# A spectral mixing block with one routed token: W's last rows by one gather, the second group's half columns on GpSimd, and seven even buffers against eight of two sizes

## The chip, the cores and the metric

The kernel runs on one core of one Trainium2 chip. Its time is the device time of one execution in microseconds: 198.0 us is the median of three runs (197.77 to 198.25). The profile is one further execution: it took 199.04 us, of which 197.4 us are the span from the first to the last instruction. Engines are called by their short names in the profile: PE (matmul), DVE (vector), ACT (scalar), POOL (GpSimd), SP (the queue that issues most loads).

## The reference

One layer over 2048 tokens of 576 numbers, all in float32:

```python
def _layernorm(x, axis=-1, eps=1e-5): ...
# mixing: Real(DFT over tokens (DFT over columns)), by dense matrices
a = einsum("bsd,ed->bse", x, dft_hid_re)
b = einsum("bsd,ed->bse", x, dft_hid_im)
y = einsum("ts,bse->bte", dft_seq_re, a) - einsum("ts,bse->bte", dft_seq_im, b)
h = x + y                          # with layernorm(x) going in
# routed part: one token, a SwiGLU of width 4608
r = layernorm(h) @ w_r
idx = argsort(-r)[:, :1]
y = (silu(x_sel @ w_gate) * (x_sel @ w_up)) @ w_down * sigmoid(r_sel)
h2 = h + layernorm(h) + (y in the row of the token)
```

The two pairs of DFT matrices are inputs like any other (2 x 16.8 MB over the tokens, 2 x 1.3 MB over the columns), and so are the three matrices of the routed part (10.6 MB each).

## The kernel before, in words

**The symmetries and their check.** The kernel computes the mixing with a part of the matrices, as far as they are mirror images of themselves, and it checks on the chip that they are: it reads the mirrored parts too, subtracts or adds, squares the differences and sums the squares. If the sum is not near zero, a general path (never taken here) computes all from new. So nearly all of the matrices is loaded, and the check is work for DVE and ACT. The token matrix ("ct") comes in blocks of 128 columns by row group j (0 to 8, and 16 - j), by part i (0 real, 1 imaginary), "plain" with nine column tiles (128 partitions x 9 x 128 float32, 576 KB) and "mirrored" with seven (448 KB, gathered in reverse order by GpSimd with an indirect load). The column matrix ("wt", called W) comes in five row blocks of 128; rows 0 to 287 are needed plain and the others mirrored.

**The stages.** X is loaded, folded and normalized (0 to 30 us). Then two groups of row groups, GROUPS = [[1,2,3,4,5],[6,7,0,8]], go through the same steps: `seq` (matmuls with ct, PE), `keep` (PSUM to the tile Z, ACT and DVE), `hid` (matmuls with W, PE), `residual` and `dot_h` (add to X, product with w_r, DVE), `spread_of` (variance, ACT), `scores` (small DVE work for each batch of tokens), `result` (rows of the output, ACT and POOL) and stores by POOL. When the scores of all tokens are known, `top`, `spread`, `token` and `row_of_token` find the token and put its row, normalized, into PSUM and into the tile `xs`. Then come the routed part's products: 9 blocks of w_gate and w_up, each with four rows of 576 a partition, are multiplied with that row on POOL (`products_on_pool`, 14 of them), DVE and ACT (sums), and PE multiplies with w_down (`down`, tile pd). `last_of_row` finishes the token's row and ACT stores it.

**The checks.** `c_check(j, i)` waits for a plain and a mirrored block of row group j and of 16 - j, and forms the differences on DVE in a half of the tile Q: `off_s` (two of 128 x 896) and `off_t` (128 x 1152). `c_half` does the same for the half columns (`off_h`: of a group's plain blocks, the left half of each column tile against the right half), for two row groups at a time. `off_w` does it for W. ACT then squares the half of Q (`square`, line 368) and frees it. Q has two halves, handed out in the order in which the checks stand in the program.

**Places.** Plain blocks that `seq` uses have fixed places in the tile D (D0, D1, D2). All others (the mirrored ones, and the plain ones of 16 - j) take the next free of the "raw" places: seven in the tile R of nine column tiles each, and those units of D that are not in use. A place is free again when DVE has read it. Loads of plain blocks are issued by SP, mirrored ones by POOL, each queue in its own order and at most eight in flight. Later the same memory is cut into 16 buffers for the blocks of the routed part (R's places 0 and 1, 2 and 3, 4 and 5 make one each).

**What sets the order.** Every step is an entry with an engine, an estimated duration and its dependencies; a list scheduler (`Plan.order`) simulates them and the instructions of each engine are written in the order that comes out, the longest remaining way first. Which place a load takes is set earlier, by the order in which `ring` is called. So a changed estimate or place moves instructions on all engines. The routed part's loads are planned over six passes, each to the buffer that is free first.

In the lines: 301 is POOL's gather, 357 SP's load of a plain block, 375, 380 and 387 are `off_s`, `off_t`, `off_h` on DVE, 403 and 405 the load of W, 422 to 427 `off_w`, 619 and 623 `residual` and `dot_h`, 661 `result`, 1200 a load of the routed part, 1228 a product on POOL, 1255 `down`. The changed kernel has the same steps some 10 to 50 lines lower: its gathers are line 311, its loads of ct 372 and of W 420 and 422, its `off_h` is 406, its squares are 383 and its `result` is 692.

## Time and profile before

| what | value |
|---|---|
| median of three runs | 198.0 us |
| the profiled execution, and its span | 199.04 us, 197.4 us |
| busy: PE, DVE, ACT, POOL | 66%, 84%, 71%, 59% of the span |
| moved by DMA | 77.81 MB, 394 GB/s over the span |

The profile gives the busy time of each engine, the chain of work that ended last, groups of equal instructions, and the DMA's rate in 40 slices or in stretches of one's choice. In the timeline a row has the start, the duration (both in us), the engine, the line of the program, and the tiles out<-in with their shapes; what stands in brackets is the idle time before the instruction and who ended it. "DMA share" is the mean busy share of the 16 DMA engines, GB/s what they moved: both are high when large transfers run, a low share means that nothing was queued, and a high share at a low rate means that the engines were busy with something that moves little.

### The profile page before, as it was taken

The numbers are of one execution on the slowest core, as the hardware profiler recorded it, in microseconds if no ns is written. First come the engines' busy times: TensorE is split into PE (matmuls) and PEld (weight loads), VectorE is DVE, ScalarE is ACT, GpSimd is POOL, SyncE is SP. The second block draws the span as 40 slices with busy tenths as digits, with TensorE's granted clock in tenths as the row PEclk, the third lists the DMA queues.
The fourth block names the chain that finished last, engine by engine and source line by source line (L and its number), as shares of the span: only waits on it lengthen the run. The fifth ranks groups of instructions, "written<-read, shape, count | busy, mean of one in ns | idle before, by whom it ended". The sixth has DMA issues, their size and how long they took to land. (4 is left out here: it accounts for less than half of the span.)

```text
span 197.4 us, 2794 instructions
## 1 busy us (share of the span) xinstructions
PE 129.6 (66%) x758; PEld 89.9 (46%) x758; DVE 166.6 (84%) x419; ACT 140.4 (71%) x259; POOL 117.2 (59%) x139
## 2 busy tenths in 40 slices
PE   0007999999999999799999986900232036263940
PEld 0005667754667788477876764700121013031430
DVE  4399996999899968999799999999947999989720
ACT  3198853684699578799389399889555999877630
POOL 6488888284637876359780000003874999999900
PEclk9999999999999999999999999975555555558797
DMA  5999999999899999999999999999999999999992
GB/s 171 408 418 412 413 409 406 411 381 330 281 405 411 411 363 402 400 410 411 416 405 414 418 424 420 426 422 412 424 431 425 420 428 424 422 431 414 412 427 99
DMA packets 14587, 77.81 MB, mean 394 GB/s; under 512 B 1951, under 2 KB 1955, under 8 KB 11239
## 3 DMA queue, kind: packets, MB, share of 16 engines
q1 hardware_dynamic: 10461, 56.56, 71.5%
q0 software_dynamic: 4096, 21.03, 26.5%
q8 instruction: 7, 0.11, 0.2%
q14 instruction: 13, 0.11, 0.1%
q10 hardware_dynamic: 10, 0.00, 0.0%
HBM read 72.86 MB, written 6.49 MB: 402 GB/s over the span
## 5 line engine op out<-in xcount | busy, mean ns | idle before, releaser
L368 ACT ACTIVATE Q<-Q 128x2944 bf16<-128x2944 bf16 (+5 forms) x26 | 55.4, 2132 | 18.5 <-DVE Q L380 8.9
L610 PE MATMUL py<-W,Z 128*128 128x289 f32 x180 | 45.4, 409 | 3.8 <-DVE X L619 3.8
L565 PE MATMUL ps<-D,XF 128*128 128x320 f32 (+3 forms) x216 | 45.0, 408 | 0.5 <-DVE Z L583 0.5
L301 POOL DMA_INDIRECT R<-in_ct_dram,ic x21 | 32.1, 1528 | 17.7 <-DVE Q L375 13.5
L610 PEld LDWEIGHTS py<-W,Z 128*128 128x128 f32 x180 | 33.6, 189 | 15.2 <-issue 4.5
L565 PEld LDWEIGHTS ps<-D,XF 128*128 128x128 f32 (+1 forms) x216 | 32.0, 172 | 13.0 <-issue 1.5
L1228 POOL TENSOR_TENSOR D<-D,Z 128x1152 f32<-128x1152 f32 x8 | 20.9, 2642 | 0.0
L676 POOL DMA_DIRECT2D out_dram<-X x1 | 0.6, 621 | 32.1 <-ACT X L661 32.1
L301 POOL DMA_INDIRECT D<-in_ct_dram,ic x11 | 13.8, 1250 | 7.6 <-DVE Q L380 4.6
L498 ACT ACTIVATE junk<-X,XT 128x576 bf16<-128x576 f32 x16 | 12.3, 771 | 7.8 <-DMA X<-in_x_dram 3.3
L1233 ACT ACTIVATE junk<-D 128x576 bf16<-128x576 f32 x20 | 13.7, 683 | 3.2 <-POOL D L1228 2.6
L1255 PE MATMUL pd<-XF,H 128*1 128x144 f32 x80 | 5.3, 439 | 14.6 <-DVE H L1247 11.3
L537 PE MATMUL fo<-W,diag 128*128 128x288 f32 (+1 forms) x8 | 4.2, 706 | 16.3 <-DVE diag L528 16.3
L375 DVE TENSOR_TENSOR Q<-R,D 128x896 bf16<-128x896 f32 x11 | 11.9, 1084 | 3.2 <-DMA D<-in_ct_dram 1.8
L387 DVE TENSOR_TENSOR Q<-D 128x640 bf16<-128x640 f32 (+3 forms) x20 | 12.8, 691 | 1.7 <-DMA W<-in_wt_dram 1.7
L380 DVE TENSOR_TENSOR Q<-R,D 128x1152 bf16<-128x1152 f32 x10 | 13.4, 1348 | 0.0
L630 ACT ACTIVATE junk<-X,TD 128x576 bf16<-128x576 f32 x16 | 12.3, 766 | 1.4 <-DVE X L619 1.3
L661 ACT ACTIVATE X<-X,BB,UP 128x576 f32<-128x576 f32 x14 | 10.8, 854 | 3.1 <-DVE BB L642 3.1
L623 DVE SCALAR_TENSOR_TENSOR junk<-X,wr 128x576 bf16<-128x576 f32 x16 | 12.1, 755 | 0.3
L375 DVE TENSOR_TENSOR Q<-D 128x896 bf16<-128x896 f32 x11 | 11.8, 1082 | 0.0
L619 DVE SCALAR_TENSOR_TENSOR X<-py,X 128x576 f32<-128x576 f32 x16 | 11.6, 748 | 0.0
L375 DVE TENSOR_TENSOR Q<-R 128x896 bf16<-128x896 f32 x10 | 10.7, 1082 | 0.1
(205 smaller groups left out, 260.8 us busy)
## 6 DMA issues: line engine op xcount, KB each, us to landing
D<-in_ct_dram SPq DMA_DIRECT2D x22, 576.0 KB
R<-in_ct_dram SPq DMA_DIRECT2D x10, 576.0 KB
D<-in_wu_dram SPq DMA_DIRECT2D x5, 1152.0 KB
D<-in_wd_dram SPq DMA_DIRECT2D x4, 1152.0 KB
R<-in_wg_dram SPq DMA_DIRECT2D x3, 1152.0 KB
D<-in_wg_dram SPq DMA_DIRECT2D x3, 1152.0 KB
out_dram<-X SPq DMA_DIRECT2D x2, 1440.0 KB
X<-in_x_dram SPq DMA_DIRECT2D x4, 576.0 KB
```

Source lines behind the costliest of these rows:

```text
L301: pool.indirect_dma_start(tile, None, view, bass.IndirectOffsetOnAxis(ap=rows, axis=0), element_offset=at)
L368: act.activation(t, t, AF.Square, accum_out=DS[0 : t.shape[0], n : n + 1])
L375: dve.tensor_tensor(o, C[j, i, True][:, 0:7, :], C[j, i, False][:, 7:0:-1, :], op=SIGN[i])
L380: dve.tensor_tensor(o, C[NK - j, i, False], C[j, i, False][:, :, ::-1], op=SIGN[i])
L387: dve.tensor_tensor(o[:, :, k::2, :], t[:, :, k::2, 0:HM], t[:, :, k::2, HM:P], op=op)
L498: act.activation(junk[:, 0:D], X[:, k, 0:D], AF.Square, bias=XT[:, n : n + 1], scale=-float(D), accum_out=VX[:, n : n + 1],)
L565: pe.matmul(cm(ZP[g, n][k % 2][p0 : p0 + m], w), XF[:, q, m0 : m0 + m], DT[g, i][:, :, k, 0:HM], start=k in (0, 1), stop=k in (6, 7),)
L610: pe.matmul(YP[GROUPS[g][c]][:, h, 0:w], Z[:, a, c * P : (c + 1) * P], w_block(a)[:, h * HD : h * HD + w], start=(a == 0), stop=(a == 4),)
L623: dve.scalar_tensor_tensor(junk2, X[:, k, 0:D], 1.0, wr, op0=OP.mult, op1=OP.mult, accum_out=TD[:, n, 0:1])
L630: act.activation(junk[:, 0:D], X[:, k, 0:D], AF.Square, bias=TD[:, n, 1:2], scale=-float(D), accum_out=VAR[:, n : n + 1],)
L1228: pool.tensor_tensor(t, t, xs.unsqueeze(1).to_broadcast([P, JW, D]), op=OP.mult)
L1233: act.activation(junk[:, 0:D], WB[w, j][:, r, :], AF.Copy, accum_out=acc[:, j + r : j + r + 1])
```

## The change

Four things, and what follows from them.

1. **W's last block.** W's plain blocks now hold rows 1 to 128 and 129 to 256 instead of 0 to 127 and 128 to 255. The rest (rows 0 and 257 to 288, plain and mirrored) comes as one gather of 128 half rows of 576 numbers, with a table of row numbers in five small POOL instructions, and two half rows by SP. Before, it was a load of 33 rows, one of 32 half rows, and later a gather of 33 mirrored rows. The check of this block is a new function, `off_wc`. A clearing of the block's tile at the start of the program falls away; so does a clearing of one entry of the old table. The layout of the folded X shifts by one column to fit.
2. **The second group's half columns.** `off_h` of the second group runs on GpSimd.
3. **Eight raw places in the same 63 column tiles.** Three have nine column tiles (0 to 2) and five have seven (3 to 7). A plain block takes only a place of nine; a mirrored one takes a place of seven or a unit of D first.
4. **Two places closed early.** From the check of row group 7, part 0, on, places 0 and 1 of R get no more loads of ct.

A gather of nine entries before a store, which turns the order of the DMA engines, becomes one of four.

```diff
-N_RAW = 7
+N_RAW, N_MAIN = 8, 3
...
+LEFT = {(7, 0): (0, 1)}
...
+        pool.memset(iw[:, 2:3], 0)
+        for c in range(2):
+            for p, n, row, step in ((0, 32, D1, 2), (32, 31 + c, D - D1, -2)):
+                pool.iota(iw[64 * c + p : 64 * c + p + n, 2:3], pattern=[[0, 1]], base=2 * row + c, channel_multiplier=step)
...
-        return RAW[:, b]
+        if b < N_MAIN:
+            return RAW[:, b]
+        at = LOW + (b - N_MAIN) * 7 * P
+        return RF[:, at : at + 7 * P].rearrange("p (k m) -> p k m", m=P)
...
+    def half_on_pool(g, c, i):
+        return g == 1
...
-            dve.tensor_tensor(o[:, :, k::2, :], t[:, :, k::2, 0:HM], t[:, :, k::2, HM:P], op=op)
+            eng = pool if half_on_pool(g, c, i) else dve
+            eng.tensor_tensor(o[:, :, k::2, :], t[:, :, k::2, 0:HM], t[:, :, k::2, HM:P], op=op)
...
-            rows = wt[n * P : n * P + (P if n < 2 else 33), :].rearrange("p (c e) -> p c e", c=2)
-            sp.dma_start(t if n < 2 else t[0:33], rows)
-            if n == 2:
-                sp.dma_start(W[name][64:96, 0, 0:D], wt[2 * P : HD, D : 2 * D])
...
+        elif n == 2:
+            sp.dma_start(W["C"][0:2, 1, 0:D], wh[1 : D + 2 : D, :])
...
+        else:
+            gather(W["C"][:, 0, 0:D], wh, iw[:, 2:3])
...
+    def off_wc(u):
+
+        c, o = W["C"][:, 0, :], Q[:, u % 2, 0 : D + 289]
+        dve.memset(o[:, 0:D], 0.0)
+        for p, op in ((0, OP.subtract), (64, OP.add)):
+            dve.tensor_tensor(o[p : p + 31, 0:D], c[p + 32 : p + 63, 0:D], c[p : p + 31, 0:D], op=op)
+        dve.tensor_copy(o[32:34, 0:D], W["C"][0:2, 1, 0:D])
+        off_e(o[:, D:], c[0:64], c[64:P])
...
-    dve.memset(W["C"], 0.0)
...
-        u = free.pop(0)
+        open_ = [b for b in free if b not in shut]
+        whole = [b for b in open_ if type(b) is tuple or b < N_MAIN]
+        u = whole[0]
+        if f == load_c and args[2]:
+            u = [*[b for b in open_ if type(b) is tuple or b >= N_MAIN], *whole][0]
+        free.remove(u)
...
-            add("DVE", 0.16 + 0.62 * m, then(off_h, g, c, m, i, u), [d for _, d in cus[i]], w)
+            add(
+                *(("POOL", 0.3 + 1.31 * m) if half_on_pool(g, c, i) else ("DVE", 0.16 + 0.62 * m)),
+                then(off_h, g, c, m, i, u), [d for _, d in cus[i]], w,
+            )
...
-    for step in "sffsffwsss":
+    for step in "sffsffwcsss":
```

The rows below are the instructions of an engine in program order; "x3" stands for three alike in a row. First SP's loads after those of X, before the change (R and D are the tiles of the places, W the column matrix):

```order
L357 DMA D<-in_ct_dram 128x1152 x10
L357 DMA R<-in_ct_dram 128x1152 x2
L357 DMA D<-in_ct_dram 128x1152
L403 DMA W<-in_wt_dram 128x2x576 x2
L403 DMA W<-in_wt_dram 33x2x576
L405 DMA W<-in_wt_dram 32x576
L357 DMA D<-in_ct_dram 128x1152
L357 DMA R<-in_ct_dram 128x1152 x2
L357 DMA D<-in_ct_dram 128x1152 x2
```

and after it:

```order
L372 DMA D<-in_ct_dram 128x1152 x10
L372 DMA R<-in_ct_dram 128x1152 x3
L420 DMA W<-in_wt_dram 128x2x576 x2
L422 DMA W<-in_wt_dram 2x576
L372 DMA D<-in_ct_dram 128x1152
L372 DMA R<-in_ct_dram 128x1152 x2
L372 DMA D<-in_ct_dram 128x1152 x2
```

The two small loads of W have become one of two rows. The four plain blocks for which a place is free from the start are the same in number, three of them now in R. The eighth place goes to a mirrored block: POOL has eight gathers into places that are free from the start where it had seven.

Second, DVE at the end of the second group, before the change (py is the sum of `hid`, X the residual stream, wr is w_r; Q<-D are the half columns):

```order
L623 SCALAR_TENSOR_TENSOR junk_126,TD<-X,wr 128x576 x2
L375 TENSOR_TENSOR Q<-D 128x896
L387 TENSOR_TENSOR Q<-D 128x2x5x64
L387 TENSOR_TENSOR Q<-D 128x2x4x64
L619 SCALAR_TENSOR_TENSOR X,TD<-py_1_799,X 128x576 x2
L387 TENSOR_TENSOR Q<-D 128x2x5x64
L387 TENSOR_TENSOR Q<-D 128x2x4x64
L619 SCALAR_TENSOR_TENSOR X,TD<-py_2_818,X 128x576
```

and POOL after it, from its last gather of ct to the first store of results (on DVE the half columns of this group are gone):

```order
L311 DMA spare<-in_x_dram,ix 4x2
L406 TENSOR_TENSOR Q<-D 128x2x5x64
L406 TENSOR_TENSOR Q<-D 128x2x4x64
L406 TENSOR_TENSOR Q<-D 128x2x5x64
L406 TENSOR_TENSOR Q<-D 128x2x4x64
L406 TENSOR_TENSOR Q<-D 128x2x5x64
L406 TENSOR_TENSOR Q<-D 128x2x4x64
L406 TENSOR_TENSOR Q<-D 128x2x5x64
L406 TENSOR_TENSOR Q<-D 128x2x4x64
L707 DMA out_dram<-X 128x1728
```

All eight instructions stand on POOL between its gathers and its stores. 

Third, ACT at the same place, before the change (Q,DS<-Q is a square of a half of Q, the last two those of the half columns):

```order
L368 ACTIVATE Q,DS<-Q 128x2304
L630 ACTIVATE junk,VAR<-X,TD 128x576
L368 ACTIVATE Q,DS<-Q 128x2304
L630 ACTIVATE junk,VAR<-X,TD 128x576
L240 ACTIVATE SD<-VAR,eps 128x6
L661 ACTIVATE X<-X,BB,UP 128x576 x14
L1056 TENSOR_LOAD cit
```

and after it:

```order
L383 ACTIVATE Q,DS<-Q 128x2304
L661 ACTIVATE junk,VAR<-X,TD 128x576
L692 ACTIVATE X<-X,BB,UP 128x576 x4
L661 ACTIVATE junk,VAR<-X,TD 128x576
L250 ACTIVATE SD<-VAR,eps 128x6
L692 ACTIVATE X<-X,BB,UP 128x576 x6
L383 ACTIVATE Q,DS<-Q 128x2304
L692 ACTIVATE X<-X,BB,UP 128x576 x4
L1106 TENSOR_LOAD cit
```

The first square now stands ahead of the first four results and the last root (SD), the second one ahead of the last four results; TENSOR_LOAD is the start of `row_of_token`.

More of the change, by code (lines that the diff above doesn't have):

```diff
@@ L877, in w_first, with wc_first @@
             LAST["SP"], d = load(
-                "SP", then(load_w, None, n), (0.59, 0.59, 0.22)[n], LAST["SP"], users["W" + "ABC"[n]]
+                "SP", then(load_w, None, n), (0.59, 0.59, 0.005)[n], LAST["SP"], users["W" + "ABC"[n]]
             )
             WL.append(d)
+    def wc_first():
+        LAST["POOL"], d = load("POOL", then(load_w, None, 5), 0.295, LAST["POOL"])
+        WC.append(d)
     def w_check():
-        for n in range(3):
-            u, d = ring("POOL", load_w, (0.59, 0.59, 0.16)[n], n + 3)
+        for n in range(2):
+            u, d = ring("POOL", load_w, 0.59, n + 3)
             q, w = qs.take()
@@ L887, in w_check, with wc_check @@
             users[u].append(o)
-            squares(q, 3 * D, o, W_ROWS[n])
+            squares(q, 3 * D, o)
             WS.append(o)
             free.append(u)
+    def wc_check():
+        q, w = qs.take()
+        WS.append(add("DVE", 2.6, then(off_wc, q), WL[2], WC, w))
+        squares(q, D + 289, WS[-1])
     ZU = {(-1, False): users["Z"], (-1, True): users["Z"]}
@@ L1010 @@
         for j in GROUPS[1]:
+            shut.update(LEFT.get((j, i), ()))
             c_check(j, i)
```

88 lines of the change are left out of this document (50 added, 38 removed).

## The prediction

> **What bounds the kernel now.** I read the DMA's rate by stretches first, since the page shows the DMA engines busy in nearly every slice. The columns are the stretch and its length, five engines' busy time with instruction counts, PE's granted clock, the mean busy share of the DMA engines, and GB/s.
>
> ```profile
> 35.00:44.00 9.00, 9.00 (x38) 5.79 (x36) 9.00 (x16) 6.97 (x6) 5.40 (x2) 1.00 1.03 400
> 44.00:48.00 4.00, 4.00 (x31) 1.99 (x29) 3.48 (x5) 2.00 (x5) 0.94 (x1) 1.00 1.04 288
> ...
> 50.50:54.00 3.50, 3.50 (x15) 2.47 (x14) 2.55 (x5) 2.91 (x3) 2.26 (x2) 1.00 0.81 237
> 54.00:72.00 18.00, 18.00 (x74) 13.41 (x73) 16.09 (x19) 15.13 (x18) 11.92 (x9) 1.00 1.02 410
> 72.00:75.00 3.00, 3.00 (x15) 2.65 (x14) 2.40 (x9) 2.04 (x3) 2.26 (x3) 1.00 1.03 316
> ...
> 100.00:150.00 50.00, 29.48 (x132) 20.58 (x131) 45.52 (x125) 37.85 (x61) 13.17 (x24) 0.80 1.01 420
> 150.00:187.50 37.50, 16.61 (x230) 8.19 (x230) 34.68 (x96) 31.61 (x88) 36.30 (x14) 0.58 1.01 422
> 187.50:193.00 5.50, 2.15 (x65) 1.62 (x64) 1.09 (x7) 1.55 (x5) 0.00 (x0) 1.00 1.02 420
> 193.00:195.00 2.00, 0.00 (x0) 0.00 (x0) 0.00 (x0) 0.00 (x0) 0.00 (x0) 1.00 0.38 138
> ```
>
> The loads run at 400 to 422 GB/s without a pause until 193 us, but for three places. In two of them (44 to 48 and 72 to 75 us) the engines are busy and move little. In the third (50.5 to 54) the share falls to 0.81: nothing was queued. So the stream of loads is a bound, and it can be shortened at those three places.
>
> Then the end, from the timeline: POOL's first and last product, PE's last instructions, the token's row and its store.
>
> ```profile
> 151.10 2.62 POOL L1228 TENSOR_TENSOR XF<-XF,Z 128x1152 f32<-128x1152 f32 x1 [2.91 <-ACT Z L1103]
> 184.73 2.67 POOL L1228 TENSOR_TENSOR D<-D,Z 128x1152 f32<-128x1152 f32 x1
> 190.56 1.16 PE L1255 MATMUL pd<-W,H 128*1 128x144 f32 x32
> 191.79 0.37 DVE L1268 SCALAR_TENSOR_TENSOR orow<-pd,sg,orow 97x144 f32<-97x144 f32 x1 [1.91 <-PE pd L1255]
> 192.30 1.12 ACTq L1278 DMA_DIRECT2D out_dram<-orow  x1
> ```
>
> Between the first product and the last POOL is busy 36.30 of 37.50 us (row 150 to 187.5 above): the 14 products stand end to end. They start when the token's row is there (the wait for ACT, Z), and the row's store follows the last of them by 192.30 - 187.40 = 4.9 us. So there is a second bound: the time at which the token is known, call it the token's time (151.1 us), plus 46.3 us. It ends together with the stream of loads. A gain needs both; the smaller of the two gains is what the end shows.
>
> **The stream of loads.** These are the issues of W's loads (SP's row of three includes the one of 33 rows; POOL's is the mirrored gather of 33 rows).
>
> ```profile
> 30.57 2.38 SPq L403 DMA_DIRECT2D W<-in_wt_dram  x3
> 64.21 0.94 POOL L301 DMA_INDIRECT D<-in_wt_dram,iw  x1 [0.30 <-issue]
> 70.64 0.76 DVE L422 TENSOR_TENSOR Q<-R,W 128x576 bf16<-128x576 f32 x1 [1.82 <-DMA R<-in_wt_dram,iw]
> 95.14 1.09 DVE L375 TENSOR_TENSOR Q<-R,D 128x896 bf16<-128x896 f32 x1 [1.77 <-DMA D<-in_ct_dram]
> 41.72 9.63 SPq L357 DMA_DIRECT2D R<-in_ct_dram  x2
> ```
>
> The gather of W's first mirrored block, issued two gathers ahead of that at 64.21, ends DVE's wait at 70.64; the small one, one gather later, falls into 72 to 75. The small plain loads are the last of W behind a queue that was some ten microseconds long, and fall into 44 to 48. I take both slow stretches to be the transfers with 33 rows. The first moved 4.0 x 288 = 1.152 MB, which at 410 GB/s takes 2.81 us: 1.19 us lost. The second moved 0.948 MB, 2.31 us: 0.69 lost. The change replaces them by a gather of 128 even rows, of the kind that ran at 410 between 54 and 72 us, and a load of two. In bytes it removes two times 33 x 1152 and 32 x 576 numbers and adds 130 x 576: 378 kB against 300 kB, 0.19 us. Sum: 1.19 + 0.69 + 0.19 = 2.07 us. The bounds are 0.2, if the slow stretches have another cause, and 2.07, if the two-row load costs nothing visible.
>
> The first 1.19 us are not safe by themselves. SP's row at 41.72 shows two loads that took 9.63 us to issue: the places were full until DVE had read them, and from 50.5 the queue was empty. If W's loads end 1.0 us earlier (1.19 less the part of the new gather, which is now issued here), the queue is empty that much earlier. But the eighth place lets one more mirrored block be fetched ahead: 128 x 896 x 4 bytes = 0.459 MB, 1.12 us at 410. It pays for just that. So the hole at 50.5 (0.83 MB in 3.5 us, 1.48 us lost) should stay as it is, and I count nothing for it; its bounds are 1.48 won and some 1.2 lost. That a plain block finds only three places in R is no restriction at first: each check takes two mirrored and one plain block and gives back the same.
>
> **The token's time.** DVE is busy without a gap from 117 us to the scores; these are its costliest groups there (busy us, mean ns).
>
> ```profile
> L623 DVE SCALAR_TENSOR_TENSOR junk<-X,wr 128x576 bf16<-128x576 f32 x15 | 11.3, 755 | 0.3
> L387 DVE TENSOR_TENSOR Q<-D 128x640 bf16<-128x640 f32 (+1 forms) x8 | 5.6, 753 | 0.0
> L619 DVE SCALAR_TENSOR_TENSOR X<-py,X 128x576 f32<-128x576 f32 x4 | 2.9, 753 | 0.0
> L1228 POOL TENSOR_TENSOR D<-D,Z 128x1152 f32<-128x1152 f32 x8 | 20.9, 2642 | 0.0
> L676 POOL DMA_DIRECT2D out_dram<-X x1 | 0.6, 621 | 32.1 <-ACT X L661 32.1
> ```
>
> The half columns leave DVE: 8 instructions, 5.6 us, some 5.4 us after the overlap of neighbours. The row of L1228 (this and the next are from the page) prices them on POOL: 2642 ns for 1152 elements of two inputs, and a pair of 640 and 512 has as many, so four pairs take 10.6 us. POOL stood idle for 32.1 us between its last gathers and its first store (L676), so there is room for them once the last checks have freed the halves of Q.
>
> How much the two disturb each other no row shows for two large instructions. The nearest are a gather on POOL beside DVE's checks, and one without:
>
> ```profile
> 88.20 4.33 POOL L301 DMA_INDIRECT R<-in_ct_dram,ic  x1 [0.30 <-issue]
> 101.56 0.94 POOL L301 DMA_INDIRECT D<-in_ct_dram,ic  x1 [0.30 <-issue]
> 88.35 1.08 DVE L375 TENSOR_TENSOR Q<-D 128x896 bf16<-128x896 f32 x1
> 89.36 1.34 DVE L380 TENSOR_TENSOR Q<-R,D 128x1152 bf16<-128x1152 f32 x1
> 90.62 1.08 DVE L375 TENSOR_TENSOR Q<-R 128x896 bf16<-128x896 f32 x1
> 91.63 0.74 DVE L583 SCALAR_TENSOR_TENSOR Z<-ps,os 128x256 f32<-128x256 f32 x2
> ```
>
> The gather ended at 92.53, 0.90 after DVE went from instructions with two inputs in SBUF to one that reads PSUM: POOL had stood still for 3.4 us. DVE's own durations do not show a loss there. So POOL can be held off by DVE; whether a large POOL instruction holds off DVE is the open price. Its bounds: nothing, and all of POOL's 10.6 us less the 2.9 us of L619, which reads PSUM: 7.7 us. I take half, 3.9 us, since every entry of L623 ends with a short readout at which POOL can get in and then hold the next. The half columns thus win 5.4 - 3.9 = 1.5 us (from 5.4 won to 2.3 lost).
>
> The Trainium skill (SBUF — State Buffer, section "SBUF: two separate sides") says that VectorE and GpSimd have one pair of ports in common, that an instruction takes it whole, and that a VectorE instruction with two SBUF inputs takes it against a GpSimd one that reads SBUF. By that rule the upper bound of 7.7 us is the price, and the token's time is 2.3 us later from this edit alone; the trace agrees as far as POOL stood still for 3.4 us.
>
> Upstream, DVE waited 1.77 us at 95.14 for a load that the shorter stream brings some 2 us earlier, and has no gap behind it: up to 1.8 us. The token's time should come 1.5 + 1.8 = 3.3 us earlier, more than the 2.07 of the loads. So the loads set the gain.
>
> **What is hidden.** `off_wc` has two instructions of 31 x 576, a clearing and a copy where `off_w` had two of 33 x 576; rows of the old block and of a clearing of 288 numbers:
>
> ```profile
> 76.97 0.74 DVE L422 TENSOR_TENSOR Q<-D,W 33x576 bf16<-33x576 f32 x1
> 79.04 0.14 DVE L427 CAST Q<-W 33x1 bf16<-33x1 f32 x1
> L698 DVE MEMSET XF<- x1: 298/298/298, 1.5 to 1.5; 128x288 f32 x1
> 10.15 0.13 POOL L222 IOTA ti<- 128x1 int32 x1
> 15.06 0.24 POOL L484 TENSOR_TENSOR DX<-X 128x4 f32<-128x4 f32 x1 [0.52 <-DMA X<-in_x_dram,ix]
> ```
>
> The same with 0.30 and a copy of at most 0.74 added: up to 1.0 us on DVE. DVE's wait at 95.14 hides it; without that cover the token is 1.0 later, which 3.3 allows. The five instructions for the new table (0.13 each, 0.65 us, one old one of the kind less) end in POOL's wait of 0.52 us at 15.06; the rest is far ahead of the first place that matters. Placing: loads of the routed part wait for D places that now POOL frees; the stream had no gap from 100 to 193 us (rows above), and a few microseconds are in its queue.
>
> **Sum.** 197.4 - 2.07 = 195.3 us of span. The execution lies 1.64 us above its span, at 199.04, and the median 1.04 below that; against the median it is 198.0 - 2.07 = 195.9, and with 0.1 for the last load, which is now two halves of 576 KB and leaves PE twice as much to do behind it, **196.0 us**.
>
> **The rivals.**
> - *The hole fills too.* The eighth place fetches far enough ahead, and 1.48 us more are won: 198.0 - 3.55 = 194.5. For it: the share of 0.81 is only a lack of places. Against it: DVE, which frees them, is busy throughout, and the token's time must come 3.5 us earlier as well.
> - *What W gives, the hole takes.* The queue is empty earlier, and the extra block is not fetched in time, since SP still waits for places in its order: only 0.69 + 0.19 = 0.88 remain, 197.1. With the lock at three quarters of its bound it comes to about the same.
> - *GpSimd and VectorE shut each other out (slower).* Each half column on POOL stops DVE's products of L623. This costs the token 7.7 - 5.4 = 2.3 us. Beside that, ACT's second square of the half columns now stands ahead of the last four results and of the token's row, and waits for POOL:
>
> ```profile
> 124.38 2.12 ACT L368 ACTIVATE Q<-Q 128x2304 bf16<-128x2304 bf16 x1 [0.19 <-DVE Q L387]
> 141.86 3.14 ACT L661 ACTIVATE X<-X,BB,UP 128x576 f32<-128x576 f32 x4 [2.40 <-DVE BB L642]
> ```
>
>   If POOL ends after 139.7, its 2.12 us delay the results. Together 4.4 us less the 1.8 from upstream, or none of it: 0.5 to 2.8 later, 199.6 in the middle. It decides from the point where POOL's eight instructions cost DVE and ACT more than 5.4 + 1.8 = 7.2 us together. Against it: DVE's instructions that read PSUM, and its waits, let POOL in.
> - *The places do not do what they say:* a plain block waits for one of three places, new holes between 55 and 100 us eat it all: 198.0.
>
> **How the numbers follow.** Forecast 43%, the hole filled 13%, the hole takes 20%, shut out 18%, places 6%. A measurement of this kernel tells 0.2%, 0.4 us, from no change. Faster: 43 + 13 + two thirds of 20, 69%. Same: 7 of the 20 and 5 of the places, 12%. Slower: 19%. The likeliest case's own range is 195.2 to 196.9; with the others 194.3 to 199.2.
>
> **What would show it.** Right: no stretch near 44 and 72 us with a full share and under 380 GB/s; a hole of about 1.5 us near 50; POOL's first product 2 us or more earlier; the stream at full rate to 191. Wrong: eight L406 that take more than 13 us in all with L654 longer than 755 ns; a first product later than 151.1; shares under 0.95 between 55 and 105 us.

## The result: 1.3% slower, and the profile after

| what | before | after |
|---|---|---|
| median, six runs of each | 198.24 us | 201.2 us |
| ratio after to before, 95% interval | | 1.0128 (1.0093 to 1.0163) |
| profiled execution, and its span | 199.04 us, 197.4 us | 200.27 us, 198.5 us |
| POOL's first product | 151.10 us | 152.72 us |
| moved by DMA | 77.81 MB | 77.74 MB |

The forecast was 196.0 us, from 194.3 to 199.2. The profiled execution of the changed kernel was the fastest of its six, so its trace shows 1.1 us of span more, where the medians are 3.0 us apart. Here and below the ratio leaves out executions in a slower state that most versions show now and then (203.39 us here), so it is not the ratio of the two medians.

The DMA's rate by stretches in the changed kernel, with the columns of the prediction:

```profile
35.00:44.00 9.00, 9.00 (x39) 5.90 (x39) 8.48 (x15) 7.39 (x8) 5.46 (x5) 1.00 1.03 406
44.00:48.00 4.00, 4.00 (x29) 2.02 (x26) 4.00 (x6) 1.08 (x4) 0.88 (x1) 1.00 1.01 393
50.50:54.00 3.50, 3.50 (x15) 2.47 (x14) 2.55 (x5) 3.50 (x3) 2.18 (x2) 1.00 1.01 388
54.00:70.00 16.00, 16.00 (x65) 11.85 (x64) 15.93 (x20) 13.75 (x17) 9.74 (x4) 1.00 1.02 409
70.00:82.00 12.00, 11.35 (x50) 9.13 (x49) 9.97 (x21) 6.84 (x14) 8.56 (x8) 1.00 0.98 343
120.00:125.00 5.00, 5.00 (x16) 3.58 (x16) 5.00 (x8) 3.38 (x8) 2.22 (x2) 0.74 0.65 234
150.00:190.00 40.00, 17.32 (x231) 8.22 (x230) 35.80 (x98) 32.48 (x90) 36.27 (x14) 0.58 1.01 421
```

and two of these stretches before the change:

```profile
70.00:82.00 12.00, 12.00 (x54) 10.07 (x54) 10.76 (x23) 9.79 (x16) 6.28 (x6) 1.00 1.02 383
120.00:125.00 5.00, 3.26 (x14) 2.25 (x13) 5.00 (x12) 4.75 (x11) 0.00 (x0) 1.00 1.02 426
```

Against 410 GB/s, the stretch at 44 to 48 us lost 1.19 us before and loses 0.17 now; the hole at 50.5 to 54 lost 1.48 and loses 0.19. That is 2.3 us won. But 70 to 82 loses 1.96 us instead of 0.79, and a new hole at 120 to 125 loses 2.15. That is 3.3 us given back: 1.0 us lost on balance.

The end, from the timeline (POOL's first product, the token's row, its store):

```profile
152.72 2.62 POOL L1282 TENSOR_TENSOR XF<-XF,Z 128x1152 f32<-128x1152 f32 x1 [3.18 <-ACT Z L1153]
193.38 0.37 DVE L1322 SCALAR_TENSOR_TENSOR orow<-pd,sg,orow 97x144 f32<-97x144 f32 x1 [1.91 <-PE pd L1309]
193.89 1.12 ACTq L1332 DMA_DIRECT2D out_dram<-orow  x1
```

The first product comes 1.62 us later, and the row's store 1.59 later. The products still stand end to end (36.27 of 40 us), and the store follows the first of them by 41.2 us as before the change, so the token's time sets the end here.

**The hole at 70 to 82 us.** The timeline of POOL and DVE ahead of it:

```profile
60.94 1.35 DVE L395 TENSOR_TENSOR Q<-R,D 128x1152 bf16<-128x1152 f32 x1
61.74 6.64 POOL L311 DMA_INDIRECT D<-in_wt_dram,iw  x1 [0.30 <-issue]
62.21 1.08 DVE L390 TENSOR_TENSOR Q<-R,D 128x896 bf16<-128x896 f32 x1
...
66.48 1.08 DVE L390 TENSOR_TENSOR Q<-R 128x896 bf16<-128x896 f32 x1
67.48 0.75 DVE L650 SCALAR_TENSOR_TENSOR X<-py,X 128x576 f32<-128x576 f32 x1
68.68 1.21 POOL L311 DMA_INDIRECT R<-in_ct_dram,ic  x1 [0.31 <-issue]
```

The gather of W's second mirrored block stood on POOL for 6.64 us instead of the usual 0.94. During that time DVE ran two checks, six instructions with two inputs in SBUF, without a pause; the gather ended 0.90 us after DVE had come to an instruction that reads PSUM. All gathers behind it were late, and with them the checks that free the places.

The wait upstream, 1.77 us at 95.14 before the change, is still there:

```profile
94.37 1.36 DVE L395 TENSOR_TENSOR Q<-R,D 128x1152 bf16<-128x1152 f32 x1 [1.37 <-DMA R<-in_ct_dram]
```

**The mutual stop and the hole at 120 to 125 us.** First the groups of the half columns on POOL and of the products with w_r on DVE (busy us, mean ns, idle before), then the timeline from the first of them:

```profile
L406 POOL TENSOR_TENSOR Q<-D 128x640 bf16<-128x640 f32 (+1 forms) x8 | 14.6, 1857 | 12.7 <-ACT Q L383 12.7
L654 DVE SCALAR_TENSOR_TENSOR junk<-X,wr 128x576 bf16<-128x576 f32 x16 | 18.1, 1131 | 0.3
```

```profile
113.17 7.57 POOL L406 TENSOR_TENSOR Q<-D 128x640 bf16<-128x640 f32 x4 [9.96 <-ACT Q L383]
113.95 2.43 DVE L390 TENSOR_TENSOR Q<-R 128x896 bf16<-128x896 f32 x1
...
117.65 1.97 DVE L654 SCALAR_TENSOR_TENSOR junk<-X,wr 128x576 bf16<-128x576 f32 x1
119.66 1.70 DVE L654 SCALAR_TENSOR_TENSOR junk<-X,wr 128x576 bf16<-128x576 f32 x1
121.30 1.08 DVE L390 TENSOR_TENSOR Q<-R,D 128x896 bf16<-128x896 f32 x1
122.40 0.33 SPq L1254 DMA_DIRECT2D R<-in_wg_dram  x1
```

DVE's products take 1131 ns in the mean instead of 755: 16 x 0.376 = 6.0 us. One check takes 2.43 us instead of 1.08. DVE thus loses 7.3 us and was relieved of 5.4. POOL needs 14.6 us instead of 10.6. The last check (121.30) frees the place that SP's next load waits for; the load is issued at 122.40, the queue behind it being empty by then. That is the hole. (The second batch shows that it takes the closed places as well.)

### The profile page after: what moved, and what is told of

It reads as the page before. It is cut to its first block, busy times and chain, and to the rows that moved or that the text cites. A ratio compares the mean times of both kernels' runs of the same rounds, so it can differ in the third digit from the quotient of the medians.

```text
span 198.5 us, 2794 instructions
## 1 busy us (share of the span) xinstructions
PE 130.9 (66%) x758; PEld 90.9 (46%) x758; DVE 168.7 (85%) x412; ACT 139.7 (70%) x259; POOL 127.0 (64%) x151
## 2 busy tenths in 40 slices
DMA packets 14483, 77.74 MB, mean 392 GB/s; under 512 B 1911, under 2 KB 1915, under 8 KB 11134
## 5 line engine op out<-in xcount | busy, mean ns | idle before, releaser
L311 POOL DMA_INDIRECT R<-in_ct_dram,ic x22 | 23.3, 1061 | 23.8 <-DVE Q L390 19.8
L406 POOL TENSOR_TENSOR Q<-D 128x640 bf16<-128x640 f32 (+1 forms) x8 | 14.6, 1857 | 12.7 <-ACT Q L383 12.7
L654 DVE SCALAR_TENSOR_TENSOR junk<-X,wr 128x576 bf16<-128x576 f32 x16 | 18.1, 1131 | 0.3
L1282 POOL TENSOR_TENSOR D<-D,Z 128x1152 f32<-128x1152 f32 x7 | 18.3, 2641 | 0.0
L390 DVE TENSOR_TENSOR Q<-R,D 128x896 bf16<-128x896 f32 x15 | 16.2, 1084 | 0.0
L311 POOL DMA_INDIRECT D<-in_ct_dram,ic x10 | 11.5, 1148 | 4.0 <-issue 1.2
L1287 ACT ACTIVATE junk<-D 128x576 bf16<-128x576 f32 x16 | 10.9, 683 | 2.8 <-POOL D L1282 2.3
L1271 DVE SCALAR_TENSOR_TENSOR junk<-R,xsp 128x576 bf16<-128x576 f32 x14 | 10.5, 751 | 0.3
L1309 PE MATMUL pd<-D,H 128*1 128x144 f32 x128 | 7.5, 400 | 4.9 <-DVE H L1301 4.9
L568 PEld LDWEIGHTS fo<-W,diag 128*128 128x128 f32 x8 | 2.5, 330 | 16.9 <-DVE diag L559 16.0
```

The costliest lines, as they stand in the source:

```text
L311: pool.indirect_dma_start(tile, None, view, bass.IndirectOffsetOnAxis(ap=rows, axis=0), element_offset=at)
L390: dve.tensor_tensor(o, C[j, i, True][:, 0:7, :], C[j, i, False][:, 7:0:-1, :], op=SIGN[i])
L406: eng.tensor_tensor(o[:, :, k::2, :], t[:, :, k::2, 0:HM], t[:, :, k::2, HM:P], op=op)
L654: dve.scalar_tensor_tensor(junk2, X[:, k, 0:D], 1.0, wr, op0=OP.mult, op1=OP.mult, accum_out=TD[:, n, 0:1])
L1282: pool.tensor_tensor(t, t, xs.unsqueeze(1).to_broadcast([P, JW, D]), op=OP.mult)
```

## Theories, and the experiments

Three theories, which are not exclusive. **First:** POOL and DVE stop each other in the second group's half columns. **Second:** W's gathers now stand where DVE runs checks without a pause, one of them is held, and a hole follows. **Third:** the two places closed early starve the loads and the checks. The uneven places were a further suspect. The first four expectations tell the theories in their own words; from the second batch on they go by number. Kernels of a batch ran on one chip beside the kernel before, whose median was 198.2 to 198.3 us in every batch. Ratios are to that kernel, with 95% intervals. Most versions have ten or twelve executions; those of 201.96, 201.48, 202.24 and 201.09 us have four.

### First batch: the half columns, and the places

The changed kernel with the half columns back on DVE:

```diff
-        return g == 1
+        return False
```

> The changed kernel with the second group's half columns back on the vector engine; W's gather, the eight places and the early closing stay. Theory 1 (GpSimd and the vector engine stop each other): in the changed kernel the eight half columns took GpSimd 14.6 us where 10.6 were reckoned, and six products of line 654 and one difference beside them took 7.3 us more than alone, against 5.4 us that left the vector engine; so here line 654 is back at 0.76 us each, the first product on GpSimd comes 1.5 to 3.5 us before 152.7, the hole in the loads at 121 to 125 us (2.2 us) is smaller, and the time is 1.5 to 3.5 us under the changed kernel, 197.5 to 199.5. Theory 2 (the places cost the time: the hole at 70 to 82 us, 2.0 us, and the places that the closing makes scarce): line 654 is back at 0.76 too, but the time stays within 1 us of the changed kernel, 200 to 202.

Measured: 201.96 us, 1.017 (1.0109 to 1.0231). Nothing was won by undoing the half columns, so the first theory alone does not explain the loss.

The kernel before with only the half columns of the second group on POOL:

```diff
-            dve.tensor_tensor(o[:, :, k::2, :], t[:, :, k::2, 0:HM], t[:, :, k::2, HM:P], op=op)
+            (pool if g == 1 else dve).tensor_tensor(o[:, :, k::2, :], t[:, :, k::2, 0:HM], t[:, :, k::2, HM:P], op=op)
```

> The kernel before with one edit: the second group's half columns on GpSimd (at the price that the changed kernel's planner has). Theory 1: they cost the vector engine 6 to 8 us beside them and take 5.4 off, and free their places later; first product 1 to 2.5 us after 151.1, time 0.5 to 2.5 us above the kernel before, with the hole near 50 us as it was. Theory 2: the half columns are worth what was reckoned or nothing; time within 0.7 us of the kernel before or under it.

Measured: 198.82 us, 1.0046 (1.0006 to 1.0085). In the order of the kernel before, the half columns lose a little and win nothing: the products with w_r take 890 ns in the mean, small instructions of the scores on DVE up to 1.57 us beside them, and POOL's first product comes at 151.70, 0.60 us later than before.

The changed kernel with seven even places:

```diff
-N_RAW, N_MAIN = 8, 3
+N_RAW, N_MAIN = 7, 7
...
-        u = whole[0]
-        if f == load_c and args[2]:
-            u = [*[b for b in open_ if type(b) is tuple or b >= N_MAIN], *whole][0]
+        u = whole[0]
```

> The changed kernel with seven even places instead of eight of two sizes; W's gather, the half columns on GpSimd and the early closing stay. Theory 1: the stop between the engines is there as in the changed kernel, so the time is 199.5 to 202; the hole near 50 us is back (1 to 2 us) or not, which the end does not see, since the token's time sets it. Theory 2: without the uneven places the time falls to 197 to 199.

Measured: 201.48 us, 1.0184 (1.0135 to 1.0233). Going back to even places wins nothing. But the trace shows that one loss was exchanged for others: no gather on POOL takes more than 1.98 us here, so the gather of 6.64 us comes with the order that the eighth place brings. In its place, 48 to 50.5 us runs at 340 GB/s and 50.5 to 54 at 290 (419 and 388 in the changed kernel), and DVE waits 2.90 us for a plain block at 95.4.

The changed kernel with POOL's half columns writing as long as before, but reading nothing. The differences of the second group's half columns are left out, so that part of the mirror check is missing:

```diff
+            if eng is pool:
+                for _ in range(3):
+                    pool.memset(o[:, :, k::2, :], 0.0)
+                continue
             eng.tensor_tensor(o[:, :, k::2, :], t[:, :, k::2, 0:HM], t[:, :, k::2, HM:P], op=op)
```

> The changed kernel in its order, but on GpSimd each half column is three clearings of the same part of Q in its place: it writes and reads nothing, so the half columns of the second group are not checked. Theory 1 (it is the two engines' reading at the same time): the products of line 654 beside them take 0.76 us, the token's time is 3 to 7 us before the changed kernel's, and the time is under 199.5. Theory 3 (it is the place in GpSimd's and the scalar engine's order and the late halves of Q): the clearings take about as long as half columns were reckoned, 1.3 us for three, and the token's time is within 1 us of the changed kernel's. If writing alone stops the vector engine too, line 654 stays near 1.5 us or more.

Measured: 198.63 us, 1.0013 (0.9972 to 1.0053). The groups of POOL's clearings and of DVE's products, and then the timeline of POOL:

```profile
L408 POOL MEMSET Q<- 128x640 bf16 (+1 forms) x24 | 13.5, 578 | 10.9 <-ACT Q L383 9.9
L658 DVE SCALAR_TENSOR_TENSOR junk<-X,wr 128x576 bf16<-128x576 f32 x16 | 12.1, 755 | 0.3
```

```profile
61.95 6.64 POOL L311 DMA_INDIRECT D<-in_wt_dram,iw  x1 [0.30 <-issue]
...
145.78 2.62 POOL L1286 TENSOR_TENSOR XF<-XF,Z 128x1152 f32<-128x1152 f32 x1 [2.81 <-ACT Z L1157]
```

POOL is busy as long (13.5 against 14.6 us), yet DVE's products are back at 755 ns and the first product comes 152.72 - 145.78 = 6.94 us earlier. So it is the reading on both engines that costs, and the first theory holds for the token: its price in this order is 6.9 us. But the time is only that of the kernel before. With the token 5.3 us earlier than there, the loads set the end (the row's store follows the first product by 45.6 us instead of 41.2), and the gather is still held 6.64 us.

### Second batch: W alone, the places, the closing

Only W's blocks (seven even places as above, and the two edits shown):

```diff
-LEFT = {(7, 0): (0, 1)}
+LEFT = {}
...
-        return g == 1
+        return False
```

> Of the change only W's blocks and their check: seven even places, none closed early, half columns on DVE. First theory (the mutual stop of DVE and POOL by the half columns is the loss, W's gather wins at 44 to 48 us): about 196.5 us, first product near 150. Second theory (W's one gather puts a whole mirrored W block on POOL at a moment when DVE runs instructions with two inputs in SBUF, the gather is held 6 us and a hole follows at 70 to 82): 199 to 200.5 us, a gather of over 6 us and a stretch under 345 GB/s there. Third theory (places 0 and 1 closed early starve the queue at 95 to 125): 197 to 198, since nothing is closed.

Measured: 200.92 us, 1.0083 (1.0037 to 1.0129). The second theory has the time about right and the reason wrong: with seven places no gather was held (the longest takes 1.98 us), and 70 to 82 us runs at 407 GB/s. What is lost instead is read in the fourth batch, where this version comes with clearings.

W's blocks and the eight places, with the same two edits:

```diff
-LEFT = {(7, 0): (0, 1)}
+LEFT = {}
...
-        return g == 1
+        return False
```

> W's blocks and eight places of two sizes; nothing closed early, half columns on DVE. First theory: about 196 us. Second theory (a held gather at 61 us): 199 to 201, hole at 70 to 82. Third theory (closed places): 196.5 to 198, and against the kernel that also closes places 0 and 1 (201.96) 4 us or more earlier, with 400 GB/s between 95 and 125.

Measured: 199.24 us, 1.0039 (0.9999 to 1.0078). The gather was held 6.63 us here too.

The changed kernel with nothing closed:

```diff
-LEFT = {(7, 0): (0, 1)}
+LEFT = {}
```

> The changed kernel, but places 0 and 1 take loads of ct to the end. First theory: no gain against the changed kernel, 200.5 to 201.5, since the eight half columns on POOL take 14.6 us as before. Second theory: the same, 200.5 to 201.5, with the hole at 70 to 82. Third theory: 198 to 199, the hole at 121 to 125 gone and the first product a microsecond earlier.

Measured: 199.29 us, 1.0038 (1.0000 to 1.0076). The closing costs 0.9% of the changed kernel's time, 1.9 us by the medians. The hole at 120 to 125 us is gone, though POOL and DVE still stop each other (the products take 991 ns):

```profile
120.00:125.00 5.00, 5.00 (x22) 3.90 (x21) 4.90 (x7) 2.59 (x6) 5.00 (x3) 1.00 1.02 426
```

It is gone as well where two places are closed and POOL reads nothing (418 GB/s in the version of 198.63 us). So the hole takes both, the closed places and the mutual stop. The token is hardly earlier (152.38 instead of 152.72).

The kernel before with nothing but two places closed:

```diff
+LEFT = {(7, 0): (0, 1)}
...
-        u = free.pop(0)
+        u = [b for b in free if b not in shut][0]
+        free.remove(u)
...
         for j in GROUPS[1]:
+            shut.update(LEFT.get((j, i), ()))
             c_check(j, i)
```

> The kernel before, but places 0 and 1 take no load of ct from the check of row group 7, part 0, on. First and second theory: 198 to 198.5. Third theory: 199.5 or more, with a stretch under 380 GB/s between 95 and 125 us that the kernel before does not have.

Measured: 199.22 us, 1.0019 (0.9978 to 1.0061). In the order of the kernel before, the closing cannot be told from no change. So what it costs depends on the order around it.

### Third batch: letting the held gather in

If the gather is held because DVE never stops reading two inputs from SBUF, a DVE instruction of one column that reads nothing should let it in. These clearings stand behind each first part of the first group's imaginary checks:

```diff
         dve.tensor_tensor(o, C[j, i, True][:, 0:7, :], C[j, i, False][:, 7:0:-1, :], op=SIGN[i])
+        if i == 1 and min(j, NK - j) in GROUPS[0]:
+            dve.memset(breath, 0.0)
```

In the changed kernel:

> The changed kernel; behind each first part of a mirrored check of the first group's imaginary blocks DVE clears one column (128x1), so that it runs no instructions with two inputs in SBUF back to back over 60 to 68 us. If the held gather (6.64 us) makes the hole at 70 to 82 us: the gather ends in under 3 us, the hole goes (400 GB/s or more in each five microseconds from 70 to 85), and since the mutual stop and the closed places stay, the time is 199 to 200.5. Rival (the hole is one of lacking places): gather short, hole stays, 201. Rival (a clearing lets nobody in): gather 6.6 as before, 201.

Measured: 200.35 us, 1.0076 (1.0035 to 1.0117). The gather in the timeline, and then two stretches:

```profile
61.42 2.36 POOL L311 DMA_INDIRECT D<-in_wt_dram,iw  x1 [0.30 <-issue]
```

```profile
70.00:82.00 12.00, 12.00 (x55) 9.94 (x54) 11.84 (x26) 7.76 (x17) 7.16 (x6) 1.00 1.02 406
...
120.00:125.00 5.00, 4.12 (x18) 2.92 (x17) 5.00 (x8) 3.35 (x9) 2.22 (x2) 1.00 0.36 96
```

A clearing of one column shortens the gather from 6.64 to 2.36 us, and the hole at 70 to 82 is gone (406 instead of 343 GB/s, 1.8 us won). The second theory holds for that hole. But the stretch at 120 to 125 falls from 234 to 96 GB/s, 1.7 us lost: the loads that stand behind the last check wait for it as before, and they now wait with an emptier queue. On DVE the gain was given back even earlier, at the wait for a plain block that took 1.37 us in the changed kernel:

```profile
94.62 1.36 DVE L398 TENSOR_TENSOR Q<-R,D 128x1152 bf16<-128x1152 f32 x1 [3.76 <-DMA R<-in_ct_dram]
```

So the checks behind it, the last one too, are as late as before, and the first product comes at 152.92.

The clearings together with POOL's half columns that read nothing:

```diff
+            dve.memset(breath, 0.0)
...
+                    pool.memset(o[:, :, k::2, :], 0.0)
```

> The same clearings, and the half columns on POOL clear three times and read nothing (their differences are left out, so the mirror check of the second group's half columns is missing). No mutual stop, no held gather. If both are the loss and the stream is what remains: no hole at 70 to 82, first product at 145 or earlier, 196 to 197 us, the predicted time. Rival (the stream keeps another hole, whatever is removed): 198 to 199.

Measured: 196.30 us, 0.9902 (0.9856 to 0.9949). The first product, and the stream from 40 to 185 us:

```profile
143.43 2.62 POOL L1289 TENSOR_TENSOR XF<-XF,Z 128x1152 f32<-128x1152 f32 x1 [2.83 <-ACT Z L1160]
```

```profile
40.00:185.00 145.00, 105.06 (x628) 72.65 (x630) 130.08 (x306) 114.46 (x206) 92.38 (x86) 0.81 1.02 416
```

With the mutual stop and the held gather away, no hole is left, and the time is near the predicted one. That is in part luck: the hole at 50.5 to 54 us, which was to stay, is gone too (401 GB/s), and the second group's half columns are not checked. The first product is 151.10 - 143.43 = 7.7 us earlier than before the change: 5.3 as in the version before with the held gather, and 2.35 more. About half of these 2.35 us is a wait: DVE waits 1.23 us for a plain block at 94.6 there and not at all here. Why it does not wait here is open: up to that point this version has the same instructions as the one before it, which waited 3.76 us.

W's blocks, eight places and the clearings, with nothing closed and the half columns on DVE (nothing is left out of the computation):

```diff
-LEFT = {(7, 0): (0, 1)}
+LEFT = {}
...
-        return g == 1
+        return False
...
+            dve.memset(breath, 0.0)
```

> W's blocks and eight places, nothing closed early, half columns on DVE, and the clearings. If the held gather is what W and the places lose: 197 to 198, under the kernel without the clearings (199.24) by 1 us or more, no hole at 70 to 82. Rival (lacking places): 199.2.

Measured: 196.52 us, 0.9903 (0.9857 to 0.9949). This is faster than both kernels, and 2.7 us less than without the clearings (better than expected).

The changed kernel with nothing closed and the clearings:

```diff
-LEFT = {(7, 0): (0, 1)}
+LEFT = {}
...
+            dve.memset(breath, 0.0)
```

> The changed kernel with nothing closed early and with the clearings. Held gather as the cause: 198 to 198.7, no hole at 70 to 82, the first product still at 151 or later because POOL and DVE stop each other. Rival (lacking places): 199.3 as without the clearings.

Measured: 199.63 us, 1.0038 (0.9990 to 1.0086), where the version before it, which differs only in having the half columns on DVE, has 196.52. I had expected 198 to 198.7. With POOL and DVE stopping each other, the clearings win nothing, although the stretch at 70 to 82 us runs at 407 GB/s: the first product comes at 152.35, without the clearings at 152.38. The token was later than the loads anyway.

### Fourth batch: the closing, the eighth place, the number

The clearings in the kernel before, as a control:

```diff
+        if i == 1 and min(j, NK - j) in GROUPS[0]:
+            dve.memset(breath, 0.0)
```

> The kernel before with the clearings alone. Its longest gathers near 60 to 80 us take 1.8 to 2 us, so if the clearings only undo what the change brought: 198 to 198.5. Rival (the clearings help by themselves, whatever the places): 196.5 to 197.3.

Measured: 198.27 us, 1.0011 (0.9983 to 1.0040). The clearings only undo what the new order of W's gathers brought: here no gather from 55 to 80 us takes more than 2.05 us, and there is nothing to win.

The version of 196.52 us with the two places closed:

```diff
-LEFT = {}
+LEFT = {(7, 0): (0, 1)}
```

> W's blocks, eight places, the clearings, half columns on DVE, and the two places closed early: only the closing differs from the version of 196.52 us. If closing two places costs by itself (fewer blocks fetched ahead): 198 to 200, with holes between 95 and 125 us. If it only cost because the loads queued behind the last check, which the mutual stop had delayed: 196 to 197, no hole at 120 to 125.

Measured: 202.24 us, 1.0230 (1.0188 to 1.0272), 5.7 us more by the medians. The closing costs by itself. PE's timeline, its granted clock by stretches (the third number from the end), and a wait of DVE for PE:

```profile
114.97 3.26 PE L644 MATMUL py<-W,Z 128*128 128x289 f32 x6 [4.21 <-DVE X L653]
```

```profile
112.00:116.00 4.00, 1.03 (x2) 0.84 (x3) 4.00 (x8) 3.42 (x3) 0.00 (x0) 0.78 1.01 426
116.00:120.00 4.00, 4.00 (x10) 2.74 (x9) 4.00 (x8) 3.90 (x11) 0.00 (x0) 0.50 1.01 408
120.00:124.00 4.00, 4.00 (x16) 3.05 (x15) 1.82 (x5) 4.00 (x8) 0.00 (x0) 0.87 1.00 398
```

```profile
123.13 0.76 DVE L653 SCALAR_TENSOR_TENSOR X<-py,X 128x576 f32<-128x576 f32 x1 [2.18 <-PE py L644]
```

The closing moves loads, and so the order of the checks: DVE's reads of py now stand behind a run of checks, and PE has to wait for them for 4.21 us. From the end of that pause PE's granted clock is 0.50 for some 6 us, and then DVE waits for PE. The holes that I had expected between 95 and 125 us are not the main thing (95 to 105 us runs at 373 GB/s, and at 351 in the profiled execution of the faster version). So the third theory holds here, by another path than I had thought: DVE's order, PE's pause, PE's clock. The path is read from this one trace. In the changed kernel the closing acts otherwise: PE's longest pause from 105 to 125 us is 1.92 us, and the loss is the hole at 120 to 125.

W's blocks and the clearings with seven even places:

```diff
-N_RAW, N_MAIN = 8, 3
+N_RAW, N_MAIN = 7, 7
...
+            dve.memset(breath, 0.0)
```

> W's blocks and the clearings with seven even places, nothing closed, half columns on DVE. If W's blocks alone win the stretch at 44 to 48 us once no gather is held: 197 to 197.5, between before and the version with eight places (196.52). If the eighth place carries the gain (the wait near 95 us): 198 to 200, with that wait over 3 us.

Measured: 201.09 us, 1.0135 (1.0099 to 1.0170). A wait on DVE, and the stretch behind it:

```profile
97.06 1.09 DVE L391 TENSOR_TENSOR Q<-D,R 128x896 bf16<-128x896 f32 x1 [5.94 <-DMA R<-in_ct_dram]
```

```profile
100.00:110.00 10.00, 8.86 (x56) 6.31 (x57) 10.00 (x16) 8.46 (x13) 3.62 (x5) 1.00 0.87 296
```

I had expected 197 to 200. With seven places DVE waits 5.94 us for a plain block and the queue runs dry behind it; no gather is held (the longest takes 2.00 us). So W's blocks by themselves lose; the eighth place takes this wait down (to 3.85 and 3.18 us in two executions), brings the held gather, and together with the clearings turns the loss into a gain.

The version of 199.63 us with only the imaginary half columns on POOL:

```diff
-        return g == 1
+        return g == 1 and i == 1
```

> As the version of 199.63 us (nothing closed, clearings), but only the imaginary half columns on POOL: four instructions in place of eight. If each half column on POOL costs DVE more than it takes from it: between 199.63 and 196.52, about 198, the products with w_r at a mean of some 870 ns. Rival (the loss comes when both squares wait for POOL, not by the number): 199.5.

Measured: 199.59 us, 1.0081 (1.0046 to 1.0115). The two groups:

```profile
L657 DVE SCALAR_TENSOR_TENSOR junk<-X,wr 128x576 bf16<-128x576 f32 x16 | 12.1, 756 | 0.4
L409 POOL TENSOR_TENSOR Q<-D 128x640 bf16<-128x640 f32 (+1 forms) x4 | 7.3, 1840 | 11.5 <-ACT Q L383 11.5
```

The time is that of eight instructions and the rival's (199.5); that the squares are the reason is not shown. The four instructions meet none of DVE's products. They meet two of its checks, which take 2.42 and 2.45 us instead of 1.08, and behind the first of them PE has a pause:

```profile
110.92 2.42 DVE L391 TENSOR_TENSOR Q<-R 128x896 bf16<-128x896 f32 x1
116.30 2.45 DVE L391 TENSOR_TENSOR Q<-D 128x896 bf16<-128x896 f32 x1
```

```profile
114.75 14.90 PE L644 MATMUL py<-W,Z 128*128 128x289 f32 x60 [3.27 <-DVE X L653]
```

The profiled execution was the fastest of its ten (197.72 us), and PE's clock stayed at 1.00 behind the pause. In the version of 202.24 us the same 60 matmuls took 17.88 us at the lower clock, 3.0 us more. A fall of the clock in the other executions could thus make up the 1.9 us that the median lies above this one. The two fastest of the ten have the highest mean clocks (0.877 and 0.868, the others 0.846 to 0.862). That is a hint only: in the improved version of the next batch the time does not follow the mean clock. So this stays open.

### Fifth batch: the improved version again

The version of 196.52 us once more, and with clearings behind the first parts of all mirrored checks:

```diff
-        if i == 1 and min(j, NK - j) in GROUPS[0]:
+        if True:
             dve.memset(breath, 0.0)
```

> The version of 196.52 us once more (W's blocks, eight places, clearings, nothing closed, half columns on DVE), for a second profile: its first was of an execution of 198.75 us, in which DVE waited 3.85 us at 94.5 us for a plain block, while most others took 196.0 to 196.8. If that wait is the difference between its executions: a profile near 196.2 shows a wait under 1.5 us there and no hole at 155 to 165; a profile over 198 shows it again. The median stays at 196.3 to 197.

> The same, with a clearing behind both first parts of all mirrored checks, not only those of the first group's imaginary blocks. If gathers of 1.7 to 2.0 us in the second group still cost something: 195.5 to 196.2, all gathers from 75 to 100 us under 1.6 us. Rival (only the one held over 6 us mattered, and each clearing costs DVE 0.1 us): 196.5 to 197.5.

Measured: 197.44 us, 0.9956 (0.9914 to 0.9997), and 197.78 us, 0.9979 (0.9942 to 1.0015). More clearings win nothing more. Over its two batches the improved version is 0.4% to 1.0% faster than the kernel before.

PE's timeline and granted clock in its two profiled executions, first the one of 198.75 us:

```profile
107.16 21.46 PE L644 MATMUL py<-W,Z 128*128 128x289 f32 x80 [2.27 <-DVE X L653]
```

```profile
104.00:108.00 4.00, 1.73 (x13) 0.98 (x10) 4.00 (x9) 3.87 (x9) 0.00 (x0) 1.00 0.94 357
108.00:112.00 4.00, 4.00 (x11) 2.87 (x10) 4.00 (x9) 3.82 (x5) 0.00 (x0) 0.57 0.99 422
```

then the one of 197.03 us:

```profile
106.70 19.77 PE L644 MATMUL py<-W,Z 128*128 128x289 f32 x80 [2.27 <-DVE X L653]
```

```profile
104.00:108.00 4.00, 1.73 (x10) 1.06 (x6) 4.00 (x9) 3.87 (x10) 0.00 (x0) 1.00 0.98 386
108.00:112.00 4.00, 4.00 (x18) 3.09 (x17) 4.00 (x9) 3.78 (x7) 0.00 (x0) 1.00 1.01 410
```

My expectations were wrong: the median is above 197, and the wait near 95 us was 3.85 us in the one execution and 3.18 in the other. What differs more is the clock. The same pause of 2.27 us was followed by a clock of 0.57 in one execution and by full speed in the other; the same 80 matmuls took 21.46 and 19.77 us. These 1.69 us are about the 1.72 us between the two executions' times and between their first products (151.78 and 150.06). The matmuls also began 0.46 us apart, so a little of both was taken up behind them.

### The comparisons side by side

Ratios to the kernel before, all with W's new blocks; a second number is the same with the clearings.

| half columns of the second group | eight places, nothing closed | eight places, two closed | seven places, nothing closed |
|---|---|---|---|
| on DVE | 1.0039; 0.9903 and 0.9956 | 1.0170; 1.0230 | 1.0083; 1.0135 |
| on POOL | 1.0038; 1.0038 | **1.0128**; 1.0076 | |
| POOL writes, reads nothing | | 1.0013; 0.9902 | |

The parts do not add up. Moving the half columns to POOL costs 0.8 to 1.4% in the first column with the clearings and nothing without them, and it wins 0.4 to 1.5% in the second, where on DVE the reads of py are late. Which wait comes last decides.

## Why the prediction was wrong, step by step

Three steps failed: W's gathers in their new place (2), the price of the half columns and the wait upstream (3), and the placing, put at nothing (5).

1. **What bounds the kernel** (loads and the token's time end together, a gain needs both): right. In the version that reads nothing on POOL the token came 5.3 us earlier and the time stayed at that of the kernel before, until the loads had lost their hole too; then it was 196.3.
2. **The loads, 2.07 us won:** the slow stretch at 44 to 48 us went as predicted (1.02 of 1.19 us). The hole at 50.5, which I expected to stay, went too: the rival of the filled hole was right there. The 0.69 us at 72 to 75 were lost again, because the new order, W's and the eighth place's together, put a gather of W where DVE runs two checks without a pause (with the clearings that stretch runs at 408 GB/s). I had quoted the row of a gather held for 4.33 us, and used it only for the half columns. *The step that failed* is that W's remaining gathers counted as costless in their new place: 1.2 us between 70 and 82.
3. **The token's time, 3.3 us earlier:** *this step failed in its price.* I took half of the bound, 3.9 us. DVE's rows show 7.3 us, and the version without reading shows 6.9. The argument for the half (POOL gets in only at DVE's readouts) was no reason for a half: the rows above show products of 1.97 and 1.70 us, one behind the other, and a check of 2.43, beside POOL's instructions of 1.9 us; getting in at a readout is enough to stop the next product. By the Trainium skill (SBUF — State Buffer, section "SBUF: two separate sides") the whole 7.7 would have been taken, and the trace agrees with that rule, also in that POOL's clearings, which read nothing, left DVE's products at 755 ns. The term upstream failed too: of DVE's wait of 1.77 us, 1.37 were still there, so 0.4 us were won and not 1.8. The rows give 7.3 - 5.4 - 0.4 = 1.5 us later; 1.6 was measured, and 3.3 earlier was forecast. What sets that wait is not shown: letting the held gather in made it 3.76 us in one version and none in another.
4. **The rival that was right** is the third, shut out: the token 0.5 to 2.8 us later was forecast (its own terms, 4.4 - 1.8, give 2.6 as the upper end), 1.6 was measured. Its signs came as named: L406 took 14.6 us, L654 1131 ns. Its time, 199.6 in the middle, was still 1.6 us short, and its second part was wrong. ACT's second square does stand ahead of the last four results, but POOL was done with the half columns at 130.6, and the square ran from 141.1 to 143.2, right behind other results. DVE had the last factors (BB) ready at 143.06, so the square pushed the results back by some 0.1 us and not by 2.12:

```profile
141.11 2.11 ACT L383 ACTIVATE Q<-Q 128x2304 bf16<-128x2304 bf16 x1
...
143.21 3.13 ACT L692 ACTIVATE X<-X,BB,UP 128x576 f32<-128x576 f32 x4
```

5. **Placing, costed at nothing:** *this step failed altogether.* I argued that the stream had no gap from 100 to 193 us and its queue held a few microseconds. The two closed places cost 0.9% in the changed kernel (0.4% with the clearings) and 3% (5.7 us by the medians) where DVE does the half columns and the clearings are in. In the changed kernel they make, together with the mutual stop, the gap at 120 to 125 us that I had ruled out: 234 GB/s with them, 426 without. In the other order they change the order of the checks, of the reads of py behind them, and so PE's pauses; no term of my sum looked there.
6. **What is hidden** (`off_wc`, the table): nothing in the traces speaks against it; no experiment measured it alone.
7. **The resolution:** 0.4 us was too fine. The intervals here reach 0.3 to 0.6% to each side, about 0.6 us or more.

What stays open: why an execution waits more or less at 95 us for the same block (0.7 us apart in one kernel, 3.8 us apart in two versions that are the same up to there); why half the half columns on POOL cost as much as all; and the part of the loss that the profiled execution of the changed kernel, its fastest, does not show.

## What to carry to other kernels

Price an instruction of two SBUF inputs on POOL, beside such work on DVE, at the whole time for which they overlap (here DVE lost 7.3 us and was relieved of 5.4), and look for gathers on POOL in any stretch where DVE runs such instructions without a pause; a one-column instruction that reads nothing can let them in. A change of places or buffers is also a change of order: look in the new order for the engine that is waited for (here DVE, whose late reads stop PE), not only at the queue of loads. When two bounds end together, removing one loss shows nothing until the other is gone, so test the removals in pairs.

## What the runs showed of the hardware

- A gather on POOL was held for 6.64 us across the ends of several DVE instructions; a clearing of 128x1 between them brought it to 2.36. So the end of a DVE instruction with two SBUF inputs does not let POOL in when the next such instruction follows at once.
- A pause of PE of 2.27 us was followed by a granted clock near 0.5 in one execution and not in another of the same kernel, at a cost of 1.69 us for 80 matmuls. The Trainium skill (TensorE: Matmul & The Clock Gate, section "Part 1: The HAM clock gate (the "warmup" mystery)") says that the clock falls to half after an idle window of some 3.4 us that runs free of the kernel. The value of a half and the dependence on chance agree with the rows; a pause shorter than the window was enough here. A longer pause, 3.27 us in the version of 199.59 us, was followed by full speed in its profiled execution.
